# Five changes of order in a tuned one-core kernel: a weight conversion, a tanh, an addition, Newton's steps and the fourth chunks' transposes

## The chip, the cores and the metric

The kernel runs on one core of a Trainium2 chip. The metric is the device time of one execution in microseconds (us), as a median over executions. The core has a matrix engine (TensorE, PE in the profile, with its weight loads as PEld), a vector engine (VectorE, DVE), an activation engine (ScalarE, ACT), GpSimd (POOL) and a queue that issues transfers (SP). Each engine has its own instructions in an order, and where one waits for another engine, those behind it wait too: in the trace of before, ScalarE stood 3.94 us until VectorE's L344 was done, and the relus behind in its order, whose products were done at 66.2, began at 70.53.

## The reference

An mLSTM cell makes `y` from `q, k, v` and three gates, for 4 batches, 8 heads, 768 steps and 40 features per head. A mixing block follows, with 320 features per step.

```python
# mLSTM, for every step t (all batches and heads)
C = f_stab * C + i_stab * outer(v_t, k_t);  n = f_stab * n + i_stab * k_t
y_t = sigmoid(o_t) * (C @ q_t) / max(|n . q_t|, 1)
# mixing block on x = y, heads side by side
u = x + real(fft(fft(x, axis=1), axis=2))
un = (u - mean(u)) / sqrt(var(u) + 1e-6)
out = u + relu(un @ w_ch1) @ w_ch2          # 320 -> 1280 -> 320
```

## The kernel before

The 768 steps are cut into six chunks of 128 per batch. All work is put into a plan, `at(slot, phase, function)`, and emitted slot by slot, by phase within a slot. The kernel lays the mLSTM and the folds of one batch beside the two-layer product of the batch before it. So a change of slot or phase alters no work: it alters the place of an instruction in its engine's order.

```python
EVAC, FILL, MAIN, FILL_PE = range(4)              # phases of a slot

class Piece:                                      # a piece of the float64 weights
    def take(self): ...                           # VectorE: exponent and mantissa bits (L344, L346)
    def convert(self):                            # ScalarE (L351, L352)
        nc.scalar.activation(out=self.e, in_=self.e, func=AF.Relu, scale=2.0**23, bias=ebias)
        nc.scalar.activation(out=self.m.bitcast(FP), in_=self.m, func=AF.Copy, scale=2.0**-20, bias=1.0)
    def join(self): ...                           # VectorE, three instructions (L358, L360, L364)

def mlstm_gather(b, c):                           # state and output of a chunk out of PSUM
    ...
    nc.scalar.activation(out=k.so, in_=k.so, func=AF.Tanh, scale=0.5)

def mlstm_turn(b, c, early):                      # transposes of a chunk's output, TensorE
    k.px = bank("px", [L, NP, L]) if early else ps_h.tile([L, NP, L], FP, name="px", tag="ph")
    ...

# in plan_mlstm, for batches 1 to 3
    t = s + (8, 8, 7, 7 if b == 1 else 5, 5, 5)[c]    # slot of the transposes
    x = t + 1                                         # slot of the finish (VectorE, last at L550)

def mix_rstd(b):                                  # 1 / sqrt(var): four VectorE instructions, then
    ...
    for _ in range(3):                            # three Newton steps of four GpSimd instructions
        nc.gpsimd.tensor_tensor(out=t, in0=y, in1=y, op=OP.mult)
        ...

# in plan_batch
    if b == 0:
        ...
        add = turn + [s_mlp, s_mlp + 4, s_mlp + 6]    # additions to x (L753), free a PSUM bank
    at(s_mlp + NFF + (2 if b > 0 else 0), FILL + 0.6, mix_rstd, b)

# (take, convert, join) of weight pieces 6 to 10
when += [((s, 0.7), (s + 1, 0.7), (s + 2, 0.6)) for s in (33, 36, 39, 42, 45)]
```

"Mask" below is GpSimd's causal mask of the weights W (L443), "qg" its scaling of the queries (L431), "weighing" VectorE's product of scores and W (L471). The "relus" are ScalarE's (L865), the "centring" takes off the mean on ScalarE (L769), and "chunk (1, 1)" is batch 1, chunk 1. TensorE's L479 multiplies the state with qg and writes a `ph` buffer. The tag "ph" has two PSUM buffers for three kinds of tiles: outputs (ph), state products (pc) and transposes (px).

Of the kernel before, what the change touches and what calls it, by code (L numbers as in the profile page):

```python
# [14 lines left out]
AF = mybir.ActivationFunctionType  # L15
OP = mybir.AluOpType
# [4 lines left out]
NT = S // L  # L21
# [5 lines left out]
NFF = DFF // L  # L27
# [17 lines left out]
def backwards(ap, start, n):  # L45

    return bass.AP(tensor=ap.tensor, offset=ap.offset + start, ap=[list(d) for d in ap.ap[:-1]] + [[-1, n]])
# [3 lines left out]
def kernel(  # L51
# [14 lines left out]
    nc = tc.nc  # L66
# [16 lines left out]
    turn = iter("3210321032120312031230123012012301023130201320132013201320123021320321")  # L83
# [38 lines left out]
    def at(slot, phase, fn, *args):  # L122
        plan.setdefault((slot, phase), []).append((fn, args))
# [7 lines left out]
    EVAC, FILL, MAIN, FILL_PE = range(4)  # L131
# [249 lines left out]
    chunks = {}  # L381
# [121 lines left out]
    def mlstm_gather(b, c):  # L503
        k = chunks[b, c]
        k.hT = hT_bufs[(b * NT + c) % 2]
        if c < NT - 1:
            for hip in range(2):
                r, m = slice(hip * 64, hip * 64 + D), slice(hip * 64, hip * 64 + D1)
                Cv = k.C_next[r, :, m]
                if b == 0:  # L510
                    nc.scalar.copy(out=Cv, in_=k.pc[r])
                elif c == 0:
                    nc.vector.tensor_copy(out=Cv, in_=k.pc[r])
                else:
                    nc.vector.tensor_tensor(out=Cv, in0=Cv, in1=k.pc[r], op=OP.add)
        if c in BACKWARDS:
            nc.scalar.copy(out=k.hT[:, :, 1:], in_=backwards(k.ph, L - 1, L - 1))
            if c > TG:
                nc.scalar.copy(out=k.hT[:, :, 0:1], in_=k.ph[:, :, 0:1])
            else:  # L520
                nc.gpsimd.tensor_copy(out=k.hT[:, :, 0:1], in_=h_first)
        else:
            for r in (slice(0, L),) if c > 0 else (slice(hip * 64, hip * 64 + D1) for hip in range(2)):
                nc.scalar.copy(out=k.hT[r], in_=k.ph[r])  # L524
            if c == 0:
                nc.gpsimd.tensor_copy(out=h_first, in_=k.hT[:, :, 0:1])
        if 0 < c < TG:
            nc.scalar.copy(out=hT_bufs[(b * NT + c - 1) % 2][:, :, 0:1], in_=k.ph[:, :, 0:1])
        nc.scalar.activation(out=k.so, in_=k.so, func=AF.Tanh, scale=0.5)

    def mlstm_turn(b, c, early):
        k = chunks[b, c]
# [24 lines left out]
    def plan_mlstm(b, s0, stride=3):  # L557
        for c in range(NT):
            s = s0 + stride * c
            if b > 0:  # L560
                t = 22 + 2 * c if b == 1 and c < 3 else s - 5
                at(t, FILL, mlstm_load, b, c)
                at(t, FILL, mlstm_load_max, b, c)
                at(t, FILL, mlstm_load_decay, b, c)
                at(s, FILL, mlstm_load_o, b, c)
            if (b, c) > (0, 0):
                at(s, FILL, mlstm_exp, b, c, 0)
                at(s + 1, FILL - 0.5, mlstm_exp, b, c, NP)
                last = (b, c) == (0, NT - 1)
                at(s - 1 if last else s, FILL_PE + (2.05 if last else 2), mlstm_scores, b, c)  # L570
                if b > 0:
                    at(s + 1, FILL, mlstm_mask, b, c)
            at(s, FILL, mlstm_scale_v, b, c)
            at(s if (b, c) == (0, 2) else s + 1, FILL + 0.1, mlstm_scale_q, b, c)
            at(s + 2, FILL, mlstm_decay, b, c)
            end = (b, c) == (0, NT - 1)
            at(s + 1 if end else s + 2, FILL - 0.4 if end else FILL, mlstm_weigh, b, c)
            at(s + 2 if end else s + 3, MAIN - 0.1 if s + 3 in slots_of_halves else FILL_PE, mlstm_from_state, b, c)
            at(s + 2 if end else s + 3, FILL_PE + (2 if end else 3), mlstm_from_chunk, b, c)
            at(s + 3, FILL_PE + 3, mlstm_to_state, b, c)  # L580
            at(s + 3 if end else s + 4, FILL, mlstm_gather, b, c)
            if b == 0:
                t, x = ((8, 11), (11, 14), (13, 14), (14, 15.5), (17, 18), (18, 21))[c]
            else:
                t = s + (8, 8, 7, 7 if b == 1 else 5, 5, 5)[c]
                x = t + 1
            at(t, FILL_PE + ((2.5 if c < 4 else 1) if b == 0 else 1), mlstm_turn, b, c, b == 0 and c < 4)
            at(x, FILL + 0.05, mlstm_finish, b, c)
# [6 lines left out]
    mixes = {}  # L595
# [187 lines left out]
    def mix_rstd(b):  # L783

        k = mixes[b]
        v = st_p.tile([L, NT], FP, name="v", tag="v")
        y = k.rstd = st_p.tile([L, NT], FP, name="rstd", tag="rstd")
        t = st_p.tile([L, NT], FP, name="t", tag="t")
        nc.vector.tensor_scalar(out=v, in0=k.u[:, :, DM + 1], scalar1=1e-6, scalar2=None, op0=OP.add)
        nc.vector.tensor_scalar(out=t.bitcast(U32), in0=v.bitcast(U32), scalar1=1, scalar2=None,  # L790
                                op0=OP.logical_shift_right)
        nc.vector.tensor_scalar(out=y.bitcast(U32), in0=t.bitcast(U32), scalar1=-1.0, scalar2=float(0x5F3759DF),
                                op0=OP.mult, op1=OP.add)
        nc.vector.tensor_scalar(out=v, in0=v, scalar1=-0.5, scalar2=None, op0=OP.mult)
        for _ in range(3):
            nc.gpsimd.tensor_tensor(out=t, in0=y, in1=y, op=OP.mult)
            nc.gpsimd.tensor_tensor(out=t, in0=t, in1=v, op=OP.mult)
            nc.gpsimd.tensor_scalar(out=t, in0=t, scalar1=1.5, scalar2=None, op0=OP.add)
            nc.gpsimd.tensor_tensor(out=y, in0=t, in1=y, op=OP.mult)

    def plan_mix(b, s0, x_done, s_feat, s_add, s_turn):
        for j in range(TG):
# [298 lines left out]

    def plan_batch(b, s_mlstm, s_mix, s_mlp):
        plan_mlstm(b, s_mlstm)
        done = [s_mlstm + 3 * (j + NT // 2) + 7 + (b == 1 and j == 0) for j in range(NT // 2)]
        assert s_mix >= done[-1] and s_mlp >= s_mix + 9
        late = [s_mlp + 2 * c for c in range(TG)]
        if b == 0:
            feat = [s_mix + 1, s_mix + 1, s_mlp + 3]
            turn = [s_mix + 2, s_mix + 3, s_mix + 4]
            add = turn + [s_mlp, s_mlp + 4, s_mlp + 6]  # L1110
            late = [s_mlp + 2, s_mlp + 5, s_mlp + 7]
        else:
            feat = [s_mix + c for c in ((3, 4, 6) if b == 1 else (3, 4, 7))]
            add = [s_mix + c for c in ((4, 4, 5, 6, 7, 7) if b == 1 else (4, 4, 5, 6, 8, 9))]
            turn = [s_mix + c for c in ((5, 6, 6) if b == 1 else (6, 7, 8))]
            late = [s_mix + c for c in ((7, 8, 8) if b == 1 else (9, 10, 10))]
            at(s_mlp, EVAC + 0.5, mlp_sums)
        plan_mix(b, s_mix, done, feat, add, turn + late)
        at(s_mlp + NFF + (2 if b > 0 else 0), FILL + 0.6, mix_rstd, b)
        plan_mlp(b, s_mlp)  # L1120

    s_mlp = 31
    plan_batch(0, 0, 22, s_mlp)
    plan_batch(1, 32, 54, s_mlp + MLP_SLOTS)
    plan_batch(2, 50, 83, s_mlp + 2 * MLP_SLOTS)
    plan_batch(3, 82, 115, s_mlp + 3 * MLP_SLOTS)
    for n in range(4):
# [4 lines left out]

    when = [((2, 0.7), (4, 0.5), (6, 0.6)), ((6, 0.7), (7, 0.5), (8, 0.6)), ((11, 0.7), (13, 0.5), (22, 0.6))]
    when += [((22, 0.7), (23, 0.7), (27, 0.6)), ((27, 0.7), (28, 0.7), (32, 0.6))]
    when += [((s, 0.7), (s + 1, 0.7), (s + 2, 0.6)) for s in (33, 36, 39, 42, 45)]
    pieces = w1_pieces + w2_pieces
    for n, (w, p) in enumerate(zip(when, pieces)):
        if n > 4:
# [125 lines left out]
```

## Time and profile before

| | before |
|---|---|
| time, median of the first three runs | 420.55 us (419.62 to 420.63) |
| span of the profiled execution | 418.1 us |
| TensorE busy | 405.1 us, idle 13.0 us |
| VectorE, ScalarE, GpSimd busy | 287.8, 188.9, 115.3 us |
| TensorE's waits that the profile lists | 1.8 us on L550 in three places; L769 1.2; relus 0.9; L753 0.5; qg 0.3 |

The page gives busy times. What counts here is a second view, the list of who waited for whom with TensorE as the waiting engine, since TensorE is busy for 405.1 of 418.1 us. The timeline then shows what was on the other engines before each wait. Its columns are start and length in us, engine, line, operation, tiles (output <- inputs), shapes and count, and in brackets the engine's idle time just before and what ended it. The prediction shows most of the places; one more is this, from the timeline of the kernel before. The addition on VectorE ends at 77.26, and only then has TensorE a bank for its next products.

```profile
76.77 0.49 DVE L753 TENSOR_TENSOR x<-x,pu 128x320 f32<-128x320 f32 x1
77.40 2.17 PE L850 MATMUL pm<-uT,w_sb 128*128 128x384 f32 x6 [0.52 <-DVE x L753]
```

### The profile page before, as it was taken

Reading aid. Unit: us, or ns where it says so; the run is one execution under the profiler, and the core shown is the slowest. Engines: PE = TensorE matmul, PEld = TensorE weight load, DVE = VectorE, ACT = ScalarE, POOL = GpSimd, SP = SyncE. Lnnn points to the kernel's source line nnn. Section 1 sums busy time; section 2 is a strip of 40 time slices with the busy share of each in tenths; the row PEclk is TensorE's granted clock in tenths of the full one; section 3 lists DMA queues with packets and bytes.
Section 4 is the critical chain, followed back from the end, with each engine's and each line's share of the span. In section 5 each row is a group of like instructions: output and inputs, shape, how many; then the busy total and the mean of one; then the engine's idle time right before and its main releaser. Section 6 shows DMA issues by size and latency. Waiting matters only on the chain.

```text
span 418.1 us, 8020 instructions
## 1 busy us (share of the span) xinstructions
PE 405.1 (97%) x2966; PEld 304.0 (73%) x2966; DVE 287.8 (69%) x682; ACT 188.9 (45%) x493; POOL 115.3 (28%) x194
## 2 busy tenths in 40 slices
PE   8999999999999999999999999989999999999997
PEld 6877454676667778767559998967559988555996
DVE  8789894767995638786874569786774686335652
ACT  6986375676661232655455413735442113355000
POOL 5564201459431520333061430333050000010000
PEclk9999999999999999999999999999999999999999
DMA  7889298467774154166200444210000000000010
GB/s 225 284 227 346 85 269 260 148 195 226 241 202 148 57 156 144 60 211 179 69 0 2 153 153 131 105 36 2 0 2 0 33 31 29 4 2 0 16 48 31
DMA packets 20549, 47.14 MB, mean 113 GB/s; under 512 B 2784, under 2 KB 9312, under 8 KB 20384
## 3 DMA queue, kind: packets, MB, share of 16 engines
q1 hardware_dynamic: 20512, 46.65, 36.5%
q8 instruction: 23, 0.38, 0.4%
q14 instruction: 14, 0.11, 0.1%
HBM read 42.52 MB, written 4.11 MB: 112 GB/s over the span
## 4 chain that ended last, share of the span: by engine, by line
PE 75%; DVE 14%; DMA 5%; ACT 2%; issue 2%; POOL 0%; DVEq 0%; ACTq 0%; POOLq 0%; SPq 0%
PE po L1031 18%; PE pm L912 16%; PE po L975 8%; PE pm L917 5%; PE ps L465 4%; PE ph L486 4%; DMA kvt<-in_kv 4%; PE ph L479 3%; PE pu L733 3%; PE pm L850 2%; DVE W L471 2%; PE px L535 2%; DMA qk<-in_qkT 2%; PE pz L702 2%; PE put L776 1%
## 5 line engine op out<-in xcount | busy, mean ns | idle before, releaser
L981 DVE SCALAR_TENSOR_TENSOR x<-po,rstd,x 128x160 f32<-128x160 f32 (+1 forms) x69 | 26.9, 394 | 41.2 <-PE po L1031 35.5
L921 DVE TENSOR_TENSOR h<-h,pm 128x384 f32<-128x384 f32 x60 | 30.6, 549 | 32.5 <-PE pm L917 19.4
L421 ACT ACTIVATE W<-W,colT 128x128 f32<-128x128 f32 x144 | 45.0, 396 | 0.0
L443 POOL TENSOR_SCALAR_AFFINE_SELECT W<-W 128x1024 f32<-128x1024 f32 x18 | 21.9, 1218 | 80.6 <-ACT W L421 56.3
L912 PE MATMUL pm<-uT,w_sb 128*128 128x384 f32 x90 | 37.5, 503 | 0.2 <-DVE uT L900 0.2
L975 PE MATMUL po<-w_sb,h 128*128 128x320 f32 x120 | 34.4, 435 | 0.0
L471 DVE TENSOR_TENSOR W<-ps,W 128x512 f32<-128x512 f32 x48 | 30.7, 680 | 4.5 <-POOL W L443 4.3
L850 PE MATMUL pm<-uT,w_sb 128*128 128x384 f32 x80 | 30.0, 500 | 1.6 <-DMA qk<-in_qkT 0.9
L781 ACT COPY uT<-put 128x384 f32<-128x384 f32 x24 | 11.2, 478 | 39.8 <-PE put L776 39.8
L975 PEld LDWEIGHTS po<-w_sb,h 128*128 128x128 f32 x120 | 22.2, 190 | 9.5 <-issue 0.8
L1031 PE MATMUL po<-T,S 128*128 128x160 f32 x180 | 27.9, 302 | 0.3 <-DVE x L981 0.3
L465 PE MATMUL ps<-qk 40*128 40x128 f32 x384 | 27.4, 282 | 0.0
L465 PEld LDWEIGHTS ps<-qk 40*128 40x128 f32 x384 | 23.7, 187 | 4.7 <-issue 0.7
L1031 PEld LDWEIGHTS po<-T,S 128*128 128x128 f32 x180 | 25.5, 190 | 1.7 <-DVE x L981 0.5
L1031 PE MATMUL po<-w_sb,h 128*128 128x160 f32 x180 | 26.4, 301 | 0.0
L1031 PEld LDWEIGHTS po<-w_sb,h 128*128 128x128 f32 x180 | 25.1, 190 | 1.3 <-DVE x L981 0.3
L431 POOL TENSOR_TENSOR qg<-qk,Gb 128x512 f32<-128x512 f32 x18 | 25.7, 1430 | 0.9 <-DMA Gb<-G_d 0.8
L486 PE MATMUL ph<-W,kvt 128*41 128x128 f32 x384 | 25.8, 277 | 0.0
L524 ACT COPY h<-ph 41x512 f32<-41x512 f32 (+1 forms) x16 | 9.3, 583 | 36.2 <-PE ph L486 36.1
L912 PEld LDWEIGHTS pm<-uT,w_sb 128*128 128x128 f32 x90 | 15.5, 189 | 13.7 <-DVE h L921 6.0
L479 PEld LDWEIGHTS ph<-qg,C 128*128 128x128 f32 x160 | 20.0, 191 | 6.3 <-issue 2.6
L479 PE MATMUL ph<-qg,C 128*128 128x128 f32 x160 | 21.6, 278 | 2.9 <-DVE x L550 1.8
(207 smaller groups left out, 845.6 us busy)
## 6 DMA issues: line engine op xcount, KB each, us to landing
W<-M_d SPq DMA_DIRECT2D x18, 512.0 KB
kvt<-in_kv SPq DMA_DIRECT2D x24, 324.0 KB
qk<-in_qkT SPq DMA_DIRECT2D x48, 160.0 KB
raw<-in_w SPq DMA_DIRECT2D x10, 640.0 KB
Gb<-G_d SPq DMA_DIRECT2D x36, 128.0 KB
so<-in_o SPq DMA_DIRECT2D x24, 160.0 KB
out<-x SPq DMA_DIRECT2D x24, 160.0 KB
ds_sb<-in_dft_s SPq DMA_DIRECT2D x1, 1155.0 KB
```

What stands on the lines that cost most here:

```text
L421: nc.scalar.activation(out=k.W[:, h, :], in_=M, func=AF.Exp, scale=-1.0, bias=colT[:, c, 0, b * H + h:b * H + h + 1])
L431: nc.gpsimd.tensor_tensor(out=k.qg, in0=k.qk[:, 0], in1=k.Gb, op=OP.mult)
L465: nc.tensor.matmul(k.ps[hip][:, p, :], k.qk[r, 1, p, :], k.qk[r, 0, p, :], start=True, stop=True)
L471: nc.vector.tensor_tensor(out=Wv, in0=k.ps[hip], in1=Wv, op=OP.mult)
L479: nc.tensor.matmul(k.ph[:, p, :], k.C[:, p, :], k.qg[:, p, :], start=(p == 0), stop=False, skip_group_check=True)
L486: nc.tensor.matmul(k.ph[hip * 64:hip * 64 + D1, p, :], k.v1[:, 2 * p + hip, :], k.W[:, 2 * p + hip, :], start=(c == 0 and p == 0), stop=Tr ...
L850: nc.tensor.matmul(k.pm[i], w1_sb[:, ch, f0:f0 + L], u[2 * ch], start=(ch == 0 and not ahead), stop=(ch == 1 and ahead), skip_group_check= ...
L912: nc.tensor.matmul(bank, w, u, start=start, stop=True, skip_group_check=True)
L921: nc.vector.tensor_tensor(out=h, in0=h, in1=bank, op=OP.add)
L975: nc.tensor.matmul(k.po, hidden(gr, f)[:, i * L:(i + 1) * L], w2_sb[:, f, :], start=(f == 0), stop=(f == NFF - 1))
L981: nc.vector.scalar_tensor_tensor(out=u, in0=po, scalar=k.rstd[:, c:c + 1], in1=u, op0=OP.mult, op1=OP.add)
L1031: nc.tensor.matmul(po, a[:, f], w[:, f], start=start and f == 0, stop=f == half - 1, skip_group_check=True)
```

## The change

Its intent is to take five things out of the way of something that TensorE waits for. In the numbering of the prediction: (1) the conversion of weight piece 6 goes behind the relus of slot 35, and its join a slot later; (2) the last early addition comes a slot sooner; (3) the tanh goes behind the centring, in batches 1 to 3; (4) Newton's steps of batch 0 go from slot 41 to slots 43, 46 and 49, and the four VectorE instructions before them to slot 43; (5) the transposes of the fourth chunk come two slots later in batches 2 and 3.

```diff
-        nc.scalar.activation(out=k.so, in_=k.so, func=AF.Tanh, scale=0.5)
+        if b == 0:
+            mlstm_tanh(b, c)
... # mlstm_tanh holds the same activation
+            if b > 0:
+                at(s + 4, FILL + 0.35, mlstm_tanh, b, c)
...
-                t = s + (8, 8, 7, 7 if b == 1 else 5, 5, 5)[c]
+                t = s + (8, 8, 7, 7, 5, 5)[c]
... # the loop of Newton's steps becomes mix_rstd_step, one step
-        done = [s_mlstm + 3 * (j + NT // 2) + 7 + (b == 1 and j == 0) for j in range(NT // 2)]
+        done = [s_mlstm + 3 * (j + NT // 2) + 7 + (b > 0 and j == 0) for j in range(NT // 2)]
...
-            add = turn + [s_mlp, s_mlp + 4, s_mlp + 6]
+            add = turn + [s_mlp, s_mlp + 4, s_mlp + 5]
...
-        at(s_mlp + NFF + (2 if b > 0 else 0), FILL + 0.6, mix_rstd, b)
+        s = s_mlp + NFF + 2
+        at(s, FILL + 0.6, mix_rstd, b)
+        for n in range(3):
+            at(s + 3 * n if b == 0 else s, FILL + 0.65, mix_rstd_step, b)
...
-    when += [((s, 0.7), (s + 1, 0.7), (s + 2, 0.6)) for s in (33, 36, 39, 42, 45)]
+    when += [((33, 0.7), (35, 0.7), (36, 0.6))] + [((s, 0.7), (s + 1, 0.7), (s + 2, 0.6)) for s in (36, 39, 42, 45)]
```

More of the change, by code (lines that the diff above doesn't have):

```diff
@@ L528, in mlstm_gather, with mlstm_tanh @@
             nc.scalar.copy(out=hT_bufs[(b * NT + c - 1) % 2][:, :, 0:1], in_=k.ph[:, :, 0:1])
-        nc.scalar.activation(out=k.so, in_=k.so, func=AF.Tanh, scale=0.5)
+        if b == 0:
+            mlstm_tanh(b, c)
+    def mlstm_tanh(b, c):
+        so = chunks[b, c].so
+        nc.scalar.activation(out=so, in_=so, func=AF.Tanh, scale=0.5)
     def mlstm_turn(b, c, early):
@@ L794, in mix_rstd, with mix_rstd_step @@
         nc.vector.tensor_scalar(out=v, in0=v, scalar1=-0.5, scalar2=None, op0=OP.mult)
-        for _ in range(3):
-            nc.gpsimd.tensor_tensor(out=t, in0=y, in1=y, op=OP.mult)
-            nc.gpsimd.tensor_tensor(out=t, in0=t, in1=v, op=OP.mult)
-            nc.gpsimd.tensor_scalar(out=t, in0=t, scalar1=1.5, scalar2=None, op0=OP.add)
-            nc.gpsimd.tensor_tensor(out=y, in0=t, in1=y, op=OP.mult)
+        k.newton = v, t
+    def mix_rstd_step(b):
+        k = mixes[b]
+        y, (v, t) = k.rstd, k.newton
+        nc.gpsimd.tensor_tensor(out=t, in0=y, in1=y, op=OP.mult)
+        nc.gpsimd.tensor_tensor(out=t, in0=t, in1=v, op=OP.mult)
+        nc.gpsimd.tensor_scalar(out=t, in0=t, scalar1=1.5, scalar2=None, op0=OP.add)
+        nc.gpsimd.tensor_tensor(out=y, in0=t, in1=y, op=OP.mult)
     def plan_mix(b, s0, x_done, s_feat, s_add, s_turn):
```

## The prediction

> **What bounds the kernel now.** I read the page first, then the list of who waited for whom with TensorE as the waiting engine, then the timeline around every entry of that list.
>
> ```profile
> span 418.1 us, 8020 instructions
> PE 405.1 (97%) x2966; PEld 304.0 (73%) x2966; DVE 287.8 (69%) x682; ACT 188.9 (45%) x493; POOL 115.3 (28%) x194
> ...
> PE ph L479 <- DVE x L550: 1.8, 3, 1.3
> PE pi L137 <- DVE rest L156: 1.2, 1, 1.2
> PE put L776 <- ACT uc L769: 1.2, 4, 0.4
> PE pm L850 <- DMA qk<-in_qkT: 0.9, 1, 0.9
> ...
> PE pm L850 <- DVE x L753: 0.5, 1, 0.5
> ...
> PE ph L479 <- POOL qg L431: 0.3, 1, 0.3
> ```
>
> TensorE is busy 405.1 of 418.1 us: all its idle time is 13.0 us. The change gives it no less to do: every matmul and transpose stays and only places in the order move. So 13.0 us (3.1%) is the ceiling, and the part of it that these moves can reach is what has to be found. The "us, times, longest" of the waits show that the idle time is in single waits of 0.1 to 1.3 us. TensorE's granted clock is 1.00, so nothing is to be had there.
>
> [...]weight loads are busy 73%, not 97%; here I use the busy time only to find where matmuls stop. [...]the trace of before has a single table load, at the start. [...]the join at L360 takes 0.82 us alone and 1.70 us at 102.19, under a GpSimd mask. So GpSimd's twelve small Newton instructions are not free for VectorE either.
>
> **Part 1, the conversion (weight piece 6) behind the relus.** Timeline of before:
>
> ```profile
> 68.64 0.49 DVE L344 TENSOR_SCALAR e<-raw 128x640 uint32<-128x640 uint32 x1 [6.17 <-DMA raw<-in_w]
> 69.17 0.83 ACT L351 ACTIVATE e<-e,ebias 128x640 uint32<-128x640 uint32 x1 [3.94 <-DVE e L344]
> 70.53 0.85 ACT L865 ACTIVATE h<-pm 128x384 f32<-128x384 f32 x2
> 71.05 0.30 PEld L850 LDWEIGHTS pm<-uT,w_sb 128*128 128x128 f32 x2 [1.51 <-ACT h L865]
> 71.05 0.91 PE L850 MATMUL pm<-uT,w_sb 128*128 128x384 f32 x2 [0.90 <-DMA qk<-in_qkT]
> ```
>
> The 0.90 us is put down to a DMA, but the weight load beside it names the truth: the relus (L865). Their products were done at 66.2, but ScalarE, which works in order, had sat since 65.23 (3.94 us) before the conversion L351, which waited for VectorE's L344, which waited 6.17 us for the weights' DMA. With the conversion one slot later the relus run at about 66.3 to 67.1 and the 0.90 us goes. The join moves from slot 35 to 36, behind the weighing and the addition, where VectorE has time before its 2.23 us idle at 84.28. Gain 0.90 us.
>
> **Part 2, the addition a slot sooner.** TensorE at 77.40 waits 0.52 us for L753 (76.77 to 77.26), which frees the PSUM bank of the features. VectorE did that addition after the join (to 74.17), the state copies and a take (75.13 to 76.02). Now it follows the addition before it, done at 71.87, and the join comes after. The addition with its copies and statistics takes 1.94 us (76.06 to 78.00), so it would end near 73.8, over 1.5 us before the bank is wanted, even with TensorE 0.9 us earlier. Gain 0.52 us.
>
> **Part 3, the tanh behind the centring.** Batches 1 to 3 have 18 tanhs of 0.48 us. Only where the centring is what TensorE waits for does it matter:
>
> ```profile
> 264.00 0.48 ACT L529 ACTIVATE so<-so 128x320 f32<-128x320 f32 x1
> 264.37 0.61 ACT L769 ACTIVATE uc<-x 128x384 f32<-128x384 f32 x1
> 265.03 0.55 PE L776 MATMUL put<-ident,uc 128*128 128x128 f32 x3 [0.42 <-ACT uc L769]
> ```
>
> The start distance of tanh and centring is 0.37 us, so 0.37 of the 0.42 us goes. At 75.31 the same pair costs TensorE 0.28 us at 76.33; with parts 1 and 3 all of that goes. The finish that reads the tanh comes at least two slots later, so no new wait. Gain 0.65 us.
>
> **Part 4, Newton's steps spread.** The twelve GpSimd instructions of batch 0 take 91.92 to 97.27 = 5.35 us, and the mask is next in GpSimd's order:
>
> ```profile
> 97.07 0.20 POOL L799 TENSOR_TENSOR rstd<-t,rstd 128x6 f32<-128x6 f32 x1
> 97.21 0.19 POOL L521 COPY h<-h_first 128x4 f32<-128x4 f32 x1
> 97.35 1.09 POOL L443 TENSOR_SCALAR_AFFINE_SELECT W<-W 128x1024 f32<-128x1024 f32 x1
> 98.41 1.28 POOL L431 TENSOR_TENSOR qg<-qk,Gb 128x512 f32<-128x512 f32 x1
> 98.48 1.29 DVE L471 TENSOR_TENSOR W<-ps,W 128x512 f32<-128x512 f32 x2 [1.88 <-POOL W L443]
> 99.74 1.16 PE L479 MATMUL ph<-qg,C 128*128 128x128 f32 x8 [0.30 <-POOL qg L431]
> ```
>
> The exps for that mask were done at 92.41, so mask and qg can run about 4 us earlier. TensorE's 0.30 us goes. More important, VectorE has no gap from 98.48 to 127.40, and its last link there, L550 ending 117.11, holds TensorE 0.17 us at 117.26. Its 1.88 us of idle time goes; the four rstd instructions (0.7 us), moved from slot 41 to 43, come into that stretch. VectorE so comes out over 1 us ahead, and the raw weights' DMA, issued after GpSimd's qg frees its buffer, is issued earlier too. Gain 0.30 + 0.17 = 0.47 us. The last step, in slot 49, is well before the first residual at 127.
>
> **Part 5, fourth chunks' transposes two slots later (batches 2 and 3).** Transposes, state products and outputs share two PSUM buffers ("ph"). Before, the order was ph3 A, pc3 B, px2 A, px3 B, ph4 A: ph4 waits until VectorE's finish has read px2.
>
> ```profile
> 184.34 1.13 PE L479 MATMUL ph<-qg,C 128*128 128x128 f32 x8 [0.38 <-DVE x L550]
> ...
> 278.32 0.49 DVE L550 TENSOR_TENSOR x<-px,so 128x320 f32<-128x320 f32 x1
> 278.96 1.13 PE L479 MATMUL ph<-qg,C 128*128 128x128 f32 x8 [1.26 <-DVE x L550]
> ```
>
> Without px3 there, ph4 takes B, free since the state addition (275.26 to 275.93). Its qg is ready at 274.93. So 0.38 + 1.26 = 1.64 us go. The transposes themselves (0.43 us) are only moved.
>
> **Sum.** 0.90 + 0.52 + 0.65 + 0.47 + 1.64 = 4.18 us. Nearly all lies on the path, because TensorE is what ends last and runs almost without gaps between these places (62.16 of 62.20 us busy from 121.8 to 184). 420.55 − 4.18 = 416.4.
>
> **Rivals.**
> (a) *VectorE takes over at the new place of px3.* ph5 now gets the buffer of px3 and waits for its finish. By my count from 285.19 to 288.78 (state addition 0.7, weighing 1.3, finish 1.65 us, 3.6 in all) the finish ends about 0.4 us before ph5 wants it; then a fold of 1.8 us and another finish stand before an addition (L921) whose bank the tail products want, with about 0.6 us to spare. Against it: the margins are positive, and batch 1 has had this order all along, where the matching wait is 0.17 us at 117.26. If it bites, 0.2 to 0.6 us in each of two batches come back: 417.2.
> (b) *In slots 36 to 38 the next wait takes over.* TensorE is to arrive 1.7 us earlier at 77.40 and then wants qg, with mask and qg on GpSimd fed by ScalarE's exps; my margin is 0.4 us. For it: VectorE, ScalarE and GpSimd all wait for the raw DMA until 68.64, which does not move. Against: the relus leave the stretch after the DMA. If it bites, up to 1 us is lost: 417.4.
> (c) *The stretch 57 to 121 is really held by VectorE and DMA*, and TensorE's lead is given back at 117. The chain that ended last does run through VectorE from 98 to 117. Then only parts 3 (0.37 of it) and 5 count, 2.0 us: 418.5. The 1.88 us that part 4 frees on VectorE speaks against it.
>
> **Range and chances.** I take 0.6 us off for (a) to (c): gain 3.6, time 416.9 us, 0.9% less. All of it without loss, with a fast run, gives 415.7. Rival (c), with (a), gives 419. The spread of the before runs is 1 us. A gain of 2% would be 8.4 us, two thirds of all idle time: hardly possible. A loss of 2% would need waits that nothing here makes.
>
> **What would show it.** In the profile after: TensorE's busy time within 1 us of 405 and the span 3 to 4.5 us shorter; no wait of L850 for relus near 71, none for L753; L479's 1.8 us for L550 down to under 0.5; L776's wait for L769 down from 1.2 to about 0.6 (batch 0's early centrings stay); GpSimd's mask right after the exps near 92. If the list shows new waits of L479 for L550 near the sixth chunks, rival (a) holds; for L431 or L471 near 78, (b); at 110 to 120, (c).

## The result, and the profile after

The changed kernel takes 416.46 us (415.66 to 417.13, four runs), beside 420.59 us for the kernel before. The ratio is 0.9906, with a 95% interval of 0.9881 to 0.9930. Ratios here are the mean time of one kernel's fast runs over that of the other's of the same rounds, so not quite the ratio of the medians that I quote. A run is fast unless it lies over 1.5% above the fastest of its kernel; all were, but for one execution below. The prediction was 416.9 us, in a range of 415.7 to 419.

Lines that follow the edit have moved: L550 is now L555, L753 is L760, L769 is L776, L776 is L783, L850 is L861, L865 is L876, L799 is L810. The page after begins like this; TensorE's idle time has fallen from 13.0 to 10.0 us.

```profile
span 414.0 us, 8020 instructions
...
PE 404.0 (98%) x2966; PEld 304.2 (73%) x2966; DVE 289.3 (70%) x682; ACT 188.8 (46%) x493; POOL 115.7 (28%) x194
```

The list of TensorE's waits after, in us in total, times, longest:

```profile
...
PE ph L479 <- POOL qg L431: 1.0, 1, 1.0
...
PE put L783 <- ACT uc L776: 0.6, 2, 0.4
...
PE po L1042 <- DVE x L992: 0.3, 1, 0.3
...
PE ph L479 <- DVE x L555: 0.2, 1, 0.2
```

The waits on the relus and on the addition are gone, the one on the centring is down from 1.2 to 0.6 us and L479's on the finish from 1.8 to 0.2 us. But its wait on qg was 0.3 us before and is now 1.0 us: at another place.

To see where the time went, I cut both traces at TensorE's own landmarks, the first products of each layer of each batch, and took the differences of their start times. Smaller steps quoted below come from the starts of one and the same matmul in two traces.

| stretch of TensorE's work | before, us | after, us | difference | parts in it |
|---|---|---|---|---|
| start to first layer, batch 0 | 57.67 | 57.45 | -0.22 | none |
| first layer, batch 0 (57 to 121 us) | 64.05 | 62.49 | -1.56 | 1, 2, 3, 4 |
| second layer, batch 0 | 58.53 | 58.53 | 0.00 | |
| first layer, batch 1 (180 to 221 us) | 40.50 | 39.89 | -0.61 | 5 |
| second layer, batch 1 | 53.23 | 52.97 | -0.26 | 3 |
| first layer, batch 2 (274 to 314 us) | 39.76 | 38.26 | -1.50 | 5 |
| the rest | 104.36 | 104.37 | +0.01 | |

Three timelines of the changed kernel answer to those of before. The first is where the relus were late: they now run 1.3 us before the take (L344) that waits for the weights' transfer.

```profile
66.02 0.87 ACT L876 ACTIVATE h<-pm 128x384 f32<-128x384 f32 x2 [1.01 <-PE pm L852]
67.36 0.49 DVE L344 TENSOR_SCALAR e<-raw 128x640 uint32<-128x640 uint32 x1 [5.11 <-DMA raw<-in_w]
```

The second is where Newton's steps were: the mask is at 91.28, and TensorE's L479 follows without a wait.

```profile
91.28 1.28 POOL L443 TENSOR_SCALAR_AFFINE_SELECT W<-W 128x1024 f32<-128x1024 f32 x1 [0.36 <-DMA Gb<-G_d]
...
98.08 1.05 PE L479 MATMUL ph<-qg,C 128*128 128x128 f32 x8
```

The third covers the two places where the tanh and the fourth chunk's transposes had been. Neither line has a bracket of 0.1 us or more for TensorE any more (0.06 us is left at 262.29).

```profile
262.29 0.55 PE L783 MATMUL put<-ident,uc 128*128 128x128 f32 x3
...
274.45 1.05 PE L479 MATMUL ph<-qg,C 128*128 128x128 f32 x8
```

And this is the new wait, in the timeline of the changed kernel:

```profile
74.49 0.82 DVE L360 SCALAR_TENSOR_TENSOR m<-raw,m 128x640 f32<-128x640 uint32 x1
74.58 1.68 POOL L443 TENSOR_SCALAR_AFFINE_SELECT W<-W 128x1024 f32<-128x1024 f32 x1
75.34 1.59 DVE L364 TENSOR_TENSOR w_sb<-m,e 128x640 f32<-128x640 f32 x1
76.23 1.83 POOL L431 TENSOR_TENSOR qg<-qk,Gb 128x512 f32<-128x512 f32 x1
78.11 1.16 PE L479 MATMUL ph<-qg,C 128*128 128x128 f32 x8 [1.02 <-POOL qg L431]
```

The join (L360, L364) now lies beside GpSimd's mask and qg. At their fastest in this kernel they take 1.09 and 1.27 us, here 1.68 and 1.83. My theory was that the two engines slow each other down here, so that qg ends 1.15 us later than it could (0.59 + 0.56) and TensorE, which came at 77.09, waits. The rival was that TensorE simply comes 2.4 us earlier than before, and mask and qg could not have been earlier anyway. The other open questions were whether the parts add up, and what holds the 0.17 us before L479 at 115.49, which I had expected to go and which stayed.

### The profile page after: what moved, and what is told of

It reads as the page before.

```text
span 414.0 us, 8020 instructions
## 1 busy us (share of the span) xinstructions
PE 404.0 (98%) x2966; PEld 304.2 (73%) x2966; DVE 289.3 (70%) x682; ACT 188.8 (46%) x493; POOL 115.7 (28%) x194
## 4 chain that ended last, share of the span: by engine, by line
PE 88%; DVE 8%; ACT 2%; POOL 1%; issue 1%; ACTq 0%; DVEq 0%
PE po L1042 18%; PE pm L923 17%; PE po L986 8%; PE pm L928 6%; PE ph L486 5%; PE pm L861 5%; PE ps L465 5%; PE ph L479 4%; PE pu L740 3%; PE px L540 2%; PE pm L852 2%; PE pz L709 2%; PE put L783 2%; PE pc L496 1%; PE pz L697 1%; DVE stats L767 1%
## 5 line engine op out<-in xcount | busy, mean ns | idle before, releaser
L861 PE MATMUL pm<-uT,w_sb 128*128 128x384 f32 x80 | 29.7, 498 | 0.1
L479 PEld LDWEIGHTS ph<-qg,C 128*128 128x128 f32 x160 | 20.2, 192 | 5.5 <-POOL qg L431 1.6
L979 ACT ACTIVATE h<-h 128x384 f32<-128x384 f32 x45 | 23.1, 521 | 2.0 <-DVE h L932 2.0
```

The source lines that it names most:

```text
L479: nc.tensor.matmul(k.ph[:, p, :], k.C[:, p, :], k.qg[:, p, :], start=(p == 0), stop=False, skip_group_check=True)
L861: nc.tensor.matmul(k.pm[i], w1_sb[:, ch, f0:f0 + L], u[2 * ch], start=(ch == 0 and not ahead), stop=(ch == 1 and ahead), skip_group_check= ...
```

## The experiments

All outputs are right. Four kernels ran on one chip per call, in three calls, each beside runs of the kernel before: 420.25, 419.83 and 419.92 us in the median. The last call holds the changed kernel once more.

### Part 1 alone

```diff
-    when += [((s, 0.7), (s + 1, 0.7), (s + 2, 0.6)) for s in (33, 36, 39, 42, 45)]
+    when += [((33, 0.7), (35, 0.7), (36, 0.6))] + [((s, 0.7), (s + 1, 0.7), (s + 2, 0.6)) for s in (36, 39, 42, 45)]
```

> The kernel before with part 1 alone (conversion and join of weight piece 6 a slot later). My sum gave part 1 its 0.90 us by itself; the step seen between the two traces was 1.06 us. Theory: parts 1 and 2 hang together. The wait for the relus near 71 (0.90 us) goes, but the join (3 instructions, about 2.4 us) now stands before the late addition in VectorE's order, so the addition L753 ends near 78.5 instead of 77.3 and TensorE's wait for it grows from 0.5 to about 1.5 us or more: total within 0.5 us of before (420.1 to 421.0). Rival (the parts add up): 0.9 to 1.1 us less, and the wait for L753 stays at 0.5 to about 1 us only by TensorE's earlier arrival.

Measured: 425.95 us, ratio 1.0136 (1.0112 to 1.0160). The direction of my theory was right and its size far off. The timeline:

```profile
76.97 1.44 DVE L344 TENSOR_SCALAR e<-raw 128x640 uint32<-128x640 uint32 x1
...
79.82 0.49 DVE L753 TENSOR_TENSOR x<-x,pu 128x320 f32<-128x320 f32 x1
80.46 4.18 PE L850 MATMUL pm<-uT,w_sb 128*128 128x384 f32 x6 [4.95 <-DVE x L753]
```

Without part 2 the join and the next piece's take both stand before the addition, and two of their instructions are drawn out beside GpSimd's mask and qg: L364 takes 1.59 us and L344 1.44 us, in place of 0.83 and 0.49. TensorE waits 4.95 us. The six products after it take 4.18 us in place of 2.17. The view by windows (length, busy time and count of each engine, then the granted TensorE clock, DMA share and GB/s) shows why:

```profile
80.46:86.60 6.14, 6.14 (x16) 4.18 (x16) 4.04 (x7) 1.23 (x4) 0.00 (x0) 0.52 0.83 252
86.60:90.00 3.40, 3.40 (x54) 2.62 (x52) 0.00 (x0) 0.00 (x0) 0.00 (x0) 1.00 0.02 5
```

The granted clock is 0.52 for 6.1 us after the wait. TensorE's lag behind the kernel before grows in that time from 3.06 to 5.96 us, so the lower clock costs 2.9 us more. The same view gives 1.00 from 74 to 78 us, 0.90 from 76.00 to 80.46 and 1.00 from 86.60 to 90.00: here the clock fell within the wait, after 78 us, and was back by 86.60. The four runs of this kernel have a mean clock of 0.991 to 0.996, the fast runs of the other experiments 0.999 or 1.000. In the kernel before, the longest wait after the start was 1.26 us, and the clock stayed at 1.00 in it and after it (277.7 to 285 us). How long a wait has to be before the clock falls, these traces do not show. Part 1 is thus worth having only together with part 2.

### Part 2 alone

```diff
-            add = turn + [s_mlp, s_mlp + 4, s_mlp + 6]
+            add = turn + [s_mlp, s_mlp + 4, s_mlp + 5]
```

> The kernel before with part 2 alone (the addition a slot sooner). Both theories: the 0.52 us wait for the addition goes, 0.5 to 0.7 us less (419.9 to 420.1). Contention theory of the new 1.02 us wait for qg at 78.11: it does not appear here, because the join stays in slot 35, where GpSimd is idle; mask and qg keep about 1.35 and 1.28 us. Early-arrival rival: TensorE comes about 0.7 us earlier at qg, whose end stays at 78.2, so no wait either; if mask and qg are slowed without the join, the contention theory is wrong about its cause.

Measured: 419.12 us, ratio 0.9973 (0.9958 to 0.9988). The wait for the addition is gone. Mask and qg take 1.09 and 1.27 us, without a wait for qg near 78: with the join left in slot 35 they are not slowed, as the contention theory says. The ratio alone would be a gain of 1.1 us, but in its trace the wait for the relus is 0.26 us and not 0.90, though nothing before it was changed, and the one near 116 is 0.40 us and not 0.17.

### Part 4 alone

```diff
-        for _ in range(3):
-            nc.gpsimd.tensor_tensor(out=t, in0=y, in1=y, op=OP.mult)
... # the step becomes a function, planned in slots 43, 46 and 49 (batch 0) or s (others)
+            at(s + 3 * n if b == 0 else s, FILL + 0.65, mix_rstd_step, b)
```

> The kernel before with part 4 alone (Newton's steps moved and spread). The wait for qg at 99.74 (0.30 us) goes, worth 0.36 us between the traces. For the wait of 0.17 us for L550 at 117.26 there are two theories. Mine of the prediction (VectorE's backlog from 98 to 117 holds it): it goes. Rival (a fixed chain after TensorE's own state product: state addition 0.7, weighing 1.2, finish 1.4 us): it stays at 0.17. Total 0.3 to 0.6 us less either way.

Measured: 419.11 us, ratio 0.9982 (0.9962 to 1.0002), which by itself does not tell it from 1. The trace tells more: the wait for qg at 99.74 is gone, and L479 still waits for L550 at 116.47, 0.26 us. So the backlog theory of my prediction did not hold. In this trace the wait for the relus is 0.04 us.

### Part 5 alone

```diff
-                t = s + (8, 8, 7, 7 if b == 1 else 5, 5, 5)[c]
+                t = s + (8, 8, 7, 7, 5, 5)[c]
```

> The kernel before with part 5 alone (fourth chunks' transposes two slots later in batches 2 and 3). Theory: both waits of L479 for L550 (0.38 and 1.26 us) go and, with the restart of TensorE after each, 0.73 + 1.41 = 2.14 us: near 418.4. The sixth chunks' L479 does not wait (the finish ends about 0.45 us before). Rival: part of it was owed to the other parts, then under 1.6 us.

Measured: 417.93 us, ratio 0.9942 (0.9927 to 0.9957). The two stretches with this part in them have 39.89 and 38.27 us, within a hundredth those of the changed kernel: 0.61 + 1.50 us less. No new wait came at the sixth chunks. The gain is the part's own. But in the stretch from 57 to 121 us, where this kernel is the kernel before, it took 64.35 us and not 64.05:

```profile
107.02 0.49 DVE L344 TENSOR_SCALAR e<-raw 128x640 uint32<-128x640 uint32 x1 [1.49 <-DMA raw<-in_w]
...
117.60 1.13 PE L479 MATMUL ph<-qg,C 128*128 128x128 f32 x8 [1.01 <-DVE x L550]
```

There was no wait for the relus at all, but VectorE waited 1.49 us for another weight piece, and L479 at 117.60 waited 1.01 us in place of 0.17. The stretch depends on when the weights land, which differs from run to run: VectorE waited 2.37 us for them at 96.24 and 1.49 us at 107.02 here, in the kernel before 0.89 us at 95.71 and not at all at 106.33.

### Part 3 alone

```diff
-        nc.scalar.activation(out=k.so, in_=k.so, func=AF.Tanh, scale=0.5)
+        if b == 0:
+            mlstm_tanh(b, c)
...
+                at(s + 4, FILL + 0.35, mlstm_tanh, b, c)
```

> The kernel before with part 3 alone (tanh behind centring in batches 1 to 3). Theory: the wait of L776 for the centring falls from 0.42 to about 0.06 us at 265 and goes at 76 (0.28 us), but there the wait for the addition, 0.52 us, takes most of it up again, since the addition does not move: 0.35 to 0.6 us less. No second table load. Rival (the tanh delays something behind it in the same slot): a new wait of TensorE on ScalarE.

Measured: 419.88 us, ratio 0.9998 (0.9984 to 1.0013): a gain below about 0.7 us, not seen in the times. In the trace the wait at 265 is 0.06 us, the stretch from 221 to 274 is 0.26 us shorter, exactly as in the changed kernel, and the wait at 76 is gone, but the wait for the addition right behind it is 0.88 in place of 0.52 us. That is the expected hand-over: alone, this part keeps only its 0.26 us.

### The join back in slot 35

```diff
-    when += [((33, 0.7), (35, 0.7), (36, 0.6))] + ...
+    when += [((33, 0.7), (35, 0.7), (35, 0.8))] + ...
```

This is the changed kernel with one edit.

> The changed kernel with the join of weight piece 6 put back to slot 35, behind its conversion: it then runs before GpSimd's mask and qg instead of at the same time. Contention theory of the new 1.02 us wait of L479 for qg: the mask (L443) near 74.6 takes 1.1 to 1.4 instead of 1.68 us and qg about 1.3 instead of 1.83 us, the wait goes, 0.8 to 1.2 us less than the changed kernel (about 415.3). Early-arrival rival: mask and qg start no earlier, so at least 0.6 us of the wait stays. Danger: the late addition then ends only about 0.5 us before its bank is wanted, so a late weights' DMA can bring a wait for L753 back.

Measured: 415.67 us, ratio 0.9894 (0.9879 to 0.9910). The timeline shows the join over before the mask begins, mask and qg at their short times, and L479 comes at 77.56 without a wait:

```profile
72.89 0.83 DVE L364 TENSOR_TENSOR w_sb<-m,e 128x640 f32<-128x640 f32 x1
74.73 1.09 POOL L443 TENSOR_SCALAR_AFFINE_SELECT W<-W 128x1024 f32<-128x1024 f32 x1
75.79 1.27 POOL L431 TENSOR_TENSOR qg<-qk,Gb 128x512 f32<-128x512 f32 x1
```

In the trace's time the mask began no earlier than in the changed kernel (74.73 here, 74.58 there), yet qg ended 1.0 us earlier (77.06, there 78.06). TensorE began its first layer 0.63 us later in this run (58.08, there 57.45), so counted from there qg ended 1.63 us earlier. Three instructions of GpSimd make 1.62 us of it: the mask (0.59), qg (0.56) and, overlooked above, the small copy before the mask (L526), which took 0.19 us here and 0.66 beside the join. The new wait was made by the overlap with the join, and the early-arrival rival falls. Counted the same way, TensorE comes past this place 1.29 us earlier than in the changed kernel. The intervals of the two ratios overlap, so this rests on the traces and not on the times. In this run's trace half of it is lost again at 115.54, where L479 waits 0.89 us after late weights (VectorE waited 1.97 us at 95.15).

### qg first

```diff
-            at(s if (b, c) == (0, 2) else s + 1, FILL + 0.1, mlstm_scale_q, b, c)
+            at(s if (b, c) in ((0, 2), (1, 1)) else s + 1, FILL + 0.1, mlstm_scale_q, b, c)
```

> The changed kernel with the scaling qg of chunk (1, 1) a slot sooner on GpSimd, before the mask. Both theories: the 1.02 us wait of L479 for qg goes, about 1.1 us less than the changed kernel (about 415.3). Contention theory: the mask alone is still slowed by the join (1.5 us or more), since only qg moves; without contention it takes 1.1 us. A new wait could be on the weighing (L471), which follows the mask: I expect none, TensorE wants it near 80.

Measured: 415.49 us, ratio 0.9897 (0.9882 to 0.9912). The wait for qg goes here too, and the mask, still beside the join, is still slow:

```profile
75.21 1.68 POOL L443 TENSOR_SCALAR_AFFINE_SELECT W<-W 128x1024 f32<-128x1024 f32 x1
```

The contention is confirmed a second time. I had expected nothing new behind the mask; in fact the weighing comes late enough that the scores near 80 take 1.54 us in place of 1.06, and these 0.48 us are lost.

### The finish before the weighing

```diff
-            at(x, FILL + 0.05, mlstm_finish, b, c)
+            at(x, FILL + (-0.05 if (b, c) == (1, 3) else 0.05), mlstm_finish, b, c)
```

This edit comes on top of qg first.

> As the run with qg first, and the finish of chunk (1, 3) before the weighing of chunk (1, 5) on VectorE. Fixed-chain theory of the wait of L479 for L550 near 115.5 (0.17 us in four runs out of six): with the weighing (1.2 us) out of the chain the wait goes, and with the restart 0.3 us more than with qg first alone. Backlog theory (VectorE late from the weights' DMA): the wait goes too where the DMA is on time, but it stays in a run in which the weights land late. No new wait on L471 in slot 50.

Measured: 415.30 us, ratio 0.9888 (0.9870 to 0.9906) by its four fast runs. The profile fell in a fifth execution, of 821.26 us, in which matmuls took nearly twice as long (0.91 us in place of 0.50 for the first layer's products), while VectorE was busy for 294.1 us, little more than the 289.3 of the changed kernel. The page of this execution has no row of TensorE's clock, so the 1.000 listed for it is no measurement. TensorE was busy for 813.6 us, twice the 404.0 of the changed kernel; after part 1's wait, at a granted clock of 0.52, the first layer's products followed each other every 0.64 us, at 1.00 every 0.32. So a clock at half throughout would fit, but is not shown. Nothing else is read from it. The kernel was therefore run again:

> The same kernel as the run with qg first and the finish before the weighing, because that one's profile fell in an execution at half matmul speed. Fast profile expected: no wait of L479 for L555 near 115 when the weights land in time (0.17 us plus restart gained, 0.3 us), no wait for qg at 78; near 80 up to 0.4 us are lost where the scores wait for the late weighing, as in the run with qg first. About 415.3 us, 1 us less than the changed kernel.

Measured: 415.18 us, ratio 0.9877 (0.9856 to 0.9898). There is no wait of L479 near 115, and TensorE gains 0.41 us there. The changed kernel's timeline shows what it had waited for:

```profile
111.19 0.48 PE L496 MATMUL pc<-vw,kvt 128*40 128x41 f32 x16
111.78 0.68 DVE L515 TENSOR_TENSOR C<-C,pc 40x164 f32<-40x164 f32 x2 [0.51 <-PE pc L496]
112.49 1.29 DVE L471 TENSOR_TENSOR W<-ps,W 128x512 f32<-128x512 f32 x2
...
115.49 1.13 PE L479 MATMUL ph<-qg,C 128*128 128x128 f32 x8 [0.17 <-DVE x L555]
```

VectorE is idle for 0.51 us until TensorE's own product pc is done, then it adds to the state, weighs and finishes, so that L479 starts 3.82 us after the end of pc (115.49 less 111.67). No backlog is needed: this chain alone gives some 0.17 us (0.17 to 0.18 us in six traces, those of before and after among them, each with 3.82 or 3.83 us). A backlog of VectorE can raise it to 1.0 us, as part 5's run showed.

### The changed kernel once more

> The changed kernel unaltered, timed beside the others of this call on the same chip: 416 to 416.8 us, ratio to before about 0.990. The 1.02 us wait of L479 for qg near 78 is there again (it comes from instruction order and contention, not from the DMA). The waits that hang on the landing of the raw weights (VectorE's L344) differ from the first trace by up to 1 us each; the wait near 115 is 0.17 us where VectorE is in time and up to 1 us where the weights are late.

Measured: 416.46 us, ratio 0.9910 (0.9888 to 0.9932). The stretches agree with the first trace to 0.06 us, and the wait for qg is again 1.03 us.

### Newton's steps together

```diff
-            at(s + 3 * n if b == 0 else s, FILL + 0.65, mix_rstd_step, b)
+            at(s, FILL + 0.65, mix_rstd_step, b)
```

> The changed kernel with all three Newton steps of batch 0 in slot 43, not spread over slots 43, 46 and 49. Theory: what counted was to take them out of the mask's way in slot 41; where they go now GpSimd has time. The next mask (L443) starts up to 2.3 us later (near 101.5 instead of 100.0), the weighing after it at about 105.3 as before, and TensorE has no new wait: same time as the changed kernel within 0.3 us. Rival (the spreading matters): the mask or the state decay comes so late that L479 or L486 near 108 waits, 0.3 us or more slower.

Measured: 416.85 us, ratio 0.9914 (0.9890 to 0.9939), beside 0.9910 for the changed kernel: no difference that the times resolve. The twelve instructions take 98.43 to 103.41, 5 us, and the next mask starts at 104.06, 3 us later relative to the start of the first layer (I had said 2.3). TensorE has no new wait at L479 near 108. It waits 0.62 us at 117.01, but there VectorE had waited 2.55 us for late weights, so this run cannot say whether spreading is worth some tenths. What counts is the move out of slot 41.

### A version that tries to beat both

This is the join back in slot 35, qg of chunk (1, 1) first and the finish of chunk (1, 3) before the weighing, together with this edit:

```diff
-            at(when[n - 2][2][0] + 1, FILL + 0.7, p.load)
+            at(when[n - 2][2][0] + 1, FILL + (-0.1 if n > 6 else 0.7), p.load)
```

> A version that tries to beat both: join back in slot 35, qg of chunk (1, 1) first, finish of chunk (1, 3) before the weighing, and the loads of the last three weight pieces issued ahead of the chunk loads of their slot, not behind them. Theory: VectorE's waits for the raw weights near 94 and 104 (0.4 and 1.2 us in the changed kernel, up to 2.4 us in others) go, so that the wait of L479 near 115 cannot rise; no waits at 78 and 80. TensorE's waits after 57 us fall to about 0.9 us (58, 262, 331, 347, 351), time about 414.6 us, 1.6 to 1.8 us less than the changed kernel. Rival: the chunk loads that now come later make the exps or the state late; then a new wait of L479 or L486 on ScalarE or GpSimd.

Measured: 414.87 us (414.48 to 415.02), ratio 0.9872 (0.9850 to 0.9893). It has the lowest median, and even its slowest run is below the fastest of the changed kernel's in the same call (415.68). From the run before with qg and the finish (0.9877) the times do not tell it apart. VectorE waits for no weights after 68.40, the waits at 78, 80 and 115 are gone, and the stretch from 57 to 121 us takes 60.79 us, against 62.49 for the changed kernel. The four edits were not separated further. The timeline of this run marks one wait of TensorE between 57 and 121 us, of 0.20 us at 57.05.

## Why the prediction was right

**What bounds the kernel.** Right. TensorE's busy time changed by 1.1 us, the span by 4.1, and outside the stretches that the change touches the traces agree to 0.02 us, apart from the start.

**The sum.** I predicted 416.9 us and got 416.46, but the good fit owes something to errors of opposite sign and to luck. The sum of waits was 4.18 us; I took off 0.6 for rivals. In fact the new wait took 1.29, and the waits that went were worth more than I counted. In all five of the waits at 71.05, 77.40, 99.74, 184.34 and 278.96 of the trace before, the start of the first matmul came later by 0.164 us more than the idle time that the profile shows (1.061 us at the wait of 0.897, 1.428 us at that of 1.264). The profile counts idle time from the end of the last matmul, but without a wait the next one starts before that end: products 0.486 us long follow each other every 0.322 us. The interval after the first matmul was longer too, by 0.07 to 0.11 us. Together this is what I call the restart, 0.24 to 0.27 us. A wait that goes gives it back too. The waits that went gave back 5.31 us in all, where I had counted 4.01 for them (4.18 without the 0.17 that stayed). Luck is the 0.22 us before the first layer, which no part touches, and that the one trace that I summed had the longest wait for the relus of five (below).

| part | predicted gain, us | measured |
|---|---|---|
| 1 and 2, with the 0.28 of part 3 at 76 | 0.90 + 0.52 + 0.28 | 1.17 + 0.76 + 0.35 between the traces; part 1 alone +5.7 us |
| 4 | 0.30 + 0.17 | 0.57 between the traces at 99.74; the 0.17 us stayed |
| 3 at 265 | 0.37 | 0.36 at the wait, 0.26 over the stretch |
| 5 | 0.38 + 1.26 = 1.64 | 0.61 + 1.50 = 2.11 |
| new wait for qg | up to 1 in rival (b) | 1.29 lost with its restart |

The first stretch closes with these: 1.17 + 0.76 + 0.35 + 0.57 - 1.29 = 1.56 us.

**Part 1.** The mechanism was right: the relus (and not the DMA that the profile names) held TensorE, and with the new order they no longer do. The mis-sized term is the 0.90 us. Five traces have the old order there, and they show waits of 0.90, 0.26, 0.04, 0.00 and 0.60 us, on average 0.36, as the weights' take started 10.97, 10.33, 10.11, 10.00 and 10.67 us after the first layer began. I had one trace and took its landing for the rule. The step "The join moves from slot 35 to 36 ... where VectorE has time" failed: I looked at VectorE's time and not at what GpSimd does at that moment, although the prediction quotes the 1.70 us of L360 under a GpSimd mask. The runs with the join back and with qg first showed that it cost the new 1.02 us. I also had it the wrong way round for Newton's instructions, "not free for VectorE": in the trace before, the join beside them kept its 0.82 us per instruction, and three of Newton's took 0.78, 0.66 and 0.81 us where most of the others took 0.20 to 0.23.

**Part 2.** Right in mechanism; the 0.52 us is 0.76 with its restart. It is more important than I wrote: it is what makes part 1 harmless.

**Part 3.** Right: the wait at 265 gave back 0.36 us in place of 0.37. Some 0.09 of it is lost again by 267, in the next transposes and products; why is not known. The 0.28 us at 76 is only gained together with part 2. The tanh's new place brought no table load: the trace after has a single one of 1.28 us at 0.80, as the trace before has.

**Part 4.** Right for qg (0.57 us with its restart). Its second half failed: VectorE "has no gap from 98.48 to 127.40, and its last link there, L550 ending 117.11, holds TensorE 0.17 us". VectorE did come out ahead, and the wait stayed, since it is a fixed chain from TensorE's own product.

**Part 5.** Right in mechanism; the two restarts (2 x 0.24 us) were not in the sum, and with them it closes: 0.38 + 0.24 = 0.62 and 1.26 + 0.24 = 1.50 us. Rival (a), VectorE at the sixth chunks, did not bite: the finish's last instruction runs from 283.68 to 284.17 and L479 starts at 284.62, a margin of 0.45 us where I had counted 0.4.

**Rivals.** (b) came, though by another way than the one I described: not that the next wait was there anyway, but that the change itself lengthened it. Of (c) only this is true: how much of TensorE's lead survives at 115 differs with the weights' landing, from 0.17 to 1.01 us of wait.

**What stays open.** The ratio's interval is about 1 us to each side, so the parts of a few tenths rest on the traces and not on the times. Why one execution ran its matmuls at half speed is not known.

## What to carry to other kernels

Where the bound engine is 97% busy, sum its single waits, each with its restart (0.24 to 0.27 us here), and call that the ceiling; but take the length of a wait that ends in a transfer from several traces, not one. When an instruction is moved, look at every engine at its new place, not only at its own: a VectorE join moved beside GpSimd's mask and scaling cost 1.02 us that no dependence shows. Parts of one change need not add up: one that won with its partner lost 5.7 us without it, with a wait of 4.95 us and a granted clock of 0.52 for 6.1 us after it.

## What the traces show of the hardware

- In the changed kernel join and mask, join and qg, and take and qg overlap, and each ended 0.14 to 0.16 us sooner than if it had waited for the other's end and then taken its time alone. The mask would have ended at 75.31 + 1.09 = 76.40 and did at 76.26; L364 at 76.26 + 0.83 = 77.09 and did at 76.93; qg at 76.93 + 1.27 = 78.20 and did at 78.06; the take's L344 at 78.06 + 0.49 = 78.55 and did at 78.41.
- The profile can name the wrong releaser: the 0.90 us at 71.05 was put down to a DMA and was ended by the relus, as the weight load beside it shows.
- A transfer's landing differs from one execution to the next: the take of the same 640 KB piece began 10.00 to 10.97 us after the first layer in five traces, 7.56 to 8.51 us after the transfer was issued.
